# DRAM copies of the inverse transform's rows laid out by output quarter, each quarter loaded by two or four transfers

## The chip, the cores and the metric

The kernel runs on one NeuronCore of a Trainium2 chip. The metric is the device time of one execution in microseconds (us). Its engines are TensorE (PE; weight loads are listed apart as PEld), VectorE (DVE), ScalarE (ACT), GpSimd (POOL) and SyncE (SP), which here only issues DMAs. POOL also issues some. The transfers of both are carried by the same 16 DMA engines.

## The reference

Two independent computations, whose outputs lie side by side in one (1, 2048, 1280) bf16 tensor.

Part A is a local attention: 32 heads of width 20, each position attending to 8 positions at distances 0, 2, ..., 14.

```python
qkv = (x @ wqkv).reshape(B, S, 3, H, Dh)
logits = einsum("bhsd,bhswd->bhsw", q, kg) * scale    # kg, vg: rows gathered at pos - 2*w
attn = softmax(where(mask, logits, -1e9))
a = einsum("bhsw,bhswd->bhsd", attn, vg).reshape(B, S, D) @ wo
```

Part B is a long convolution, done by Fourier transforms, with a kernel that is generated from the parameters, and a skip term:

```python
K = einsum("dn,dnl,dn->dl", Cc, exp(logdA[:, :, None] * l), dB).real
y = irfft(rfft(u, padded to 2L) * rfft(K, padded to 2L))[:L]
b = y + u * Dskip
```

## The kernel before, in words

Part B's 640 channels are five chunks of 128 (`NCH = 5`, index c). The outer loop of `body` runs over c. In each turn DVE, PE and ACT generate one chunk's convolution kernel (four `unit`s), while the chunk before goes through its transform (`transform`), the product with the input's spectrum (`products`, L357) and the first half of the inverse transform (`inverse_a`, L373). The second half is done for all channels at the end, by the class `Inverse` (L653).

Between the two halves the data go through DRAM, since the second half needs the rows in another order:

- `inverse_a` has a tile Z of 128 partitions x 4096 bf16 for chunk c; after its fourth piece SP issues one DMA (L386) that writes it to `Zd[c]`, 8 KB in a row for each partition. A row is (real or imaginary, l0, ut), and l0 has 64 values, of which a *quarter* is 16.
- `times_d` (L391), ten times, multiplies half a chunk of the input by the skip factor on DVE and SP writes it to `UDd[c]` (L397), 2 KB in a row for each partition.
- `Inverse.load(qr, c0, c1)` (L666) fills the tile of quarter qr: 96 partitions (32 real, 32 imaginary, 32 skip rows) x 4 groups g x 5 chunks x 16 l0 x 32. For every chunk it issues three DMAs of 128 KB, each to 32 partitions, in rows of 1 KB: fifteen for a quarter. For quarters 0 and 3 they alternate between SP and POOL (8 and 7), for quarters 1 and 2 all go to SP.
- `Inverse.part` (L676) takes 2 or 3 values of l0: PE multiplies the quarter's rows by the table HB into `ps_ib`, ACT copies that to a row buffer `ysb` (four of them), and after every eighth l0 SP writes the buffer out in four DMAs (L690). There are 24 parts, six for a quarter.

A planner orders the instructions of each engine by modelled costs, except where the program pins them: `keep_in_program_order`, `issue_after`, and, from `att.in_order()` (L833) on, every matmul and ACT copy. Each engine then works its list in order; what it needs from others it waits for on semaphores. The transfers that SP issues take eight semaphores in turn.

The end of the program, from about 353 us, is a hand-written order: six `GROUPS` (L845) of eight steps `av_step` (L608), the attention-weighted sum over V. In each step DVE makes a product and PE adds it up in `ps_o`. Between the steps lie parts of the inverse, pieces of the output projection (`out_piece`, L631), and the loads of quarters 2 and 3, which `LOADS` (L846) puts at step numbers 8 * group + w: one chunk at each of the steps 4, 6, ..., 22. Parts 12 to 17 use quarter 2, parts 18 to 23 quarter 3, and the first of these stand in group 2 (step 21) and group 3 (step 31).

The tiles of the quarters take over space: quarter 0 a pool that opens when the transform's pool closes, quarter 1 the space of kT (free after the last `products` of the attention), quarter 2 that of `prod`, quarter 3 that of xT (free after the last `proj_v`).

Of the kernel before, what the change touches and what calls it, by code (L numbers as in the profile page):

```python
# [13 lines left out]
bf16 = mybir.dt.bfloat16  # L14
f32 = mybir.dt.float32

NCH = 5
# [355 lines left out]
def inverse_a(tc, pools, C, P1, P2, Zd, pool):  # L373

    nc = tc.nc
    MM = nc.tensor.matmul
    Z = pool.tile([128, 128, 32], bf16, name="Z", tag="sp", bufs=3)

    def piece(b):
        ps = pools["psum"].tile([128, 8, 128], f32, name="ps_ia", tag="bank2")  # L380
        for j in range(8):
            for w, P in enumerate((P1, P2)):
                MM(ps[:, j], lhsT=P[:, 8 * b + j].rearrange("p k g -> p (k g)"), rhs=C["EA"][:, w, :], start=(j % 4 == 0 and w == 0), stop=(w == 1), skip_group_check=True)
        nc.scalar.copy(out=Z[:, :, 8 * b:8 * b + 8], in_=ps[:].rearrange("p j x -> p x j"))
        if b == 3:
            nc.sync.dma_start(out=Zd, in_=Z[:].rearrange("p x j -> p (x j)"))  # L386

    return [lambda b=b: piece(b) for b in range(4)]


def times_d(tc, pools, C, UDd, c, i):  # L391

    nc = tc.nc
    U = C["U"][:].rearrange("p l (ut c) -> p c l ut", c=NCH)[:, c]
    UD = pools["tabb"].tile([128, 32, 32], bf16, name="UD", tag="UD")
    tc.keep_in_program_order(nc.vector.tensor_tensor(out=UD[:], in0=U[:, 32 * i:32 * i + 32], in1=bc(C["Dsb"][:, c], 1, 32), op=A.mult))
    nc.sync.dma_start(out=UDd[c, :, 1024 * i:1024 * i + 1024], in_=UD[:].rearrange("p l j -> p (l j)"))  # L397


def fwd_u(tc, pools, C, Sd, c):  # L400
# [252 lines left out]
class Inverse:  # L653
# [12 lines left out]
    def load(self, qr, c0=0, c1=NCH):  # L666
        nc = self.nc
        pool, tag = ((self.a2, "Z"), (self.att.ta, "LPC"), (self.att.a1, "prod"), (self.att.ta, "U"))[qr]
        if c0 == 0:
            self.t[qr] = pool.tile([96, 4, NCH, 16, 32], bf16, name="Z", tag=tag)  # L670
        for c in range(c0, c1):
            for ri in range(3):
                src = self.UDd[c, :, 512 * qr:512 * qr + 512] if ri == 2 else self.Zd[c, :, 2048 * ri + 512 * qr:2048 * ri + 512 * qr + 512]
                (nc.sync, nc.gpsimd)[(c + ri) % 2 if qr in (0, 3) else 0].dma_start(out=self.t[qr][32 * ri:32 * ri + 32, :, c].rearrange("p g l n -> p g (l n)"), in_=src.rearrange("(g p) n -> p g n" if ri == 2 else "(p g) n -> p g n", g=4))

    def part(self, l0, n):  # L676
        nc = self.nc
# [18 lines left out]
def body(tc, ctx, pools, prm, B_u, B_Dskip, Sd, Zd, UDd, A_x, A_wqkv, A_wo, out_a, out_b):  # L696
    nc = tc.nc
# [4 lines left out]
    fp = fft.enter_context(tc.tile_pool(name="fft", bufs=1, side="right"))  # L702
# [51 lines left out]
    LAST = NCH - 1  # L754
    for c in range(NCH):
        Kb[c] = (fp, pools["tabb"])[c % 2].tile([128, 32, 64], bf16, name="Ksb", tag="Ksb")
        F, G, Xs = small_half(tc, pools, B["cT"][:, c], R[c], *trig[c, 0][:2], 0)
        if c > 0:
            transform(c - 1)
        trig[c, 1] = trig_half(tc, pools, B, c, 1)  # L760
        unit(c, 0, 0, F, G, Xs[0])
        if c > 0:
            P1, P2, last = products(tc, pools, Sk[c - 1], Sd[c - 1], fp, True)
            ia = inverse_a(tc, pools, C, P1, P2, Zd[c - 1], fp)
            ia[0]()
        unit(c, 0, 1, F, G, Xs[1])
        if c > 0:
            for f in ia[1:]:
                f()
        if c < LAST:  # L770
            last_u = fwd_u(tc, pools, C, Sd, c if c == 0 else c + 1)
            if c == 0:
                first_u = last_u
        if c == LAST:
            att.open_k()
            for ct in range(5):
                att.proj_k(0, ct)
            att.k_halo()
        with ExitStack() as order:
            if c > 0:  # L780
                order.enter_context(tc.issue_after(last.ins))
            F, G, Xs = small_half(tc, pools, B["cT"][:, c], R[c], *trig[c, 1][:2], 1)
        if c < LAST:
            with tc.issue_after(trig[c, 1][2].ins):
                B["coefficients"](c + 1, psg)
                R[c + 1] = exps_chunk(tc, pools, B, c + 1)
            trig[c + 1, 0] = trig_half(tc, pools, B, c + 1, 0)
        else:
            att.open_q0()
        with ExitStack() as order:  # L790
            if c == 0:
                order.enter_context(tc.issue_after(first_u.ins))
            unit(c, 1, 0, F, G, Xs[0])
        if c == 0:
            fwd_u(tc, pools, C, Sd, 1)
        unit(c, 1, 1, F, G, Xs[1], q_first if c == LAST else lambda: None)
        if c == LAST - 1:
            att.load_x()
# [9 lines left out]
        if w == 3:  # L808
            transform(LAST)
    P1, P2, _ = products(tc, pools, Sk[LAST], Sd[LAST], fp, False)  # L810
    ia = inverse_a(tc, pools, C, P1, P2, Zd[LAST], fp)
    att.softmax_a(0)
    for ct in range(5):
        att.proj_q(1, ct)
# [4 lines left out]
    fft.close()  # L819
    a2 = ctx.enter_context(tc.tile_pool(name="a2", bufs=1, side="right", reuse_waits="tile"))  # L820
    inv = Inverse(att, a2, Zd, UDd, out_b)
    inv.load(0)
    att.open_v()
    for w in range(W):
        if w >= 2:
# [17 lines left out]

    att.open_out(a2)
    GROUPS = ((0, 256, 0, 2, None), (0, 128, 2, 3, 0), (128, 128, 2, 3, 1), (256, 128, 0, 4, None), (256, 256, 4, 1, 2), (384, 128, 0, 4, 3))  # L845
    LOADS = {4 + 2 * n: (2 + n // NCH, n % NCH) for n in range(2 * NCH)}  # L846
    for group, (i0, ni, j0, nj, done) in enumerate(GROUPS):
        for w in range(W):
            if group == 0:
                fill(parts, (0, 2, 0, 2, 0, 1, 0, 1)[w])  # L850
                if w == 3:
                    att.exp(1)
                if w in (0, 3):
                    att.proj_v(16 + 2 * (w == 3))
                if w == 5:
                    att.v_halo(8, 12)
            att.av_step(i0, ni, j0, nj, w)
            if 8 * group + w in LOADS:
                qr, c = LOADS[8 * group + w]
                inv.load(qr, c, c + 1)  # L860
            if 8 * group + w in (6, 8, 11, 14):
                n = (6, 8, 11, 14).index(8 * group + w)
                att.sums(2 * n, 2 * n + 2)
            if group == 0:
                if w == 2:
                    att.softmax_a(1)
                elif w == 7:
                    att.open_wo()
            elif group == 1:
                if w in (3, 5, 7):  # L870
                    fill(parts, 2)
            elif group == 2:
                if w == 1:
                    fill(rest, 3)
                elif w == 3:
                    att.reciprocal()
                    att.softmax_b(1)
                    fill(rest, 5)
                elif w in (5, 7):
                    fill(parts, 2)  # L880
            elif group < 5:
                if w % 2 == 1:
                    fill((rest, parts)[w // 2 % 2], 2)
            elif w % 2 == 1:
                fill(rest, 2)
        if done is not None:
            rest += att.out_proj(done, done == 3)
# [4 lines left out]
@with_exitstack  # L892
def kernel(
    ctx: ExitStack,
    tc: tile.TileContext,
    A_x: bass.AP,
    A_wqkv: bass.AP,
    A_wo: bass.AP,
    B_u: bass.AP,
    B_A_re: bass.AP,  # L900
    B_A_im: bass.AP,
    B_B_re: bass.AP,
    B_B_im: bass.AP,
    B_C_re: bass.AP,
    B_C_im: bass.AP,
    B_log_dt: bass.AP,
    B_Dskip: bass.AP,
    out: bass.AP,
):
    nc = tc.nc  # L910
    prm = dict(B_A_re=B_A_re, B_A_im=B_A_im, B_B_re=B_B_re, B_B_im=B_B_im, B_C_re=B_C_re, B_C_im=B_C_im, B_log_dt=B_log_dt)
    out_a = out[0][:, 0:640]
    out_b = out[0][:, 640:1280]
    pools = {}
    pools["const"] = ctx.enter_context(tc.tile_pool(name="const", bufs=1))
    idc = nc.inline_tensor(np.eye(128, dtype=np.float32).astype(ml_dtypes.bfloat16), name="ident_c")
    ident = pools["const"].tile([128, 128], bf16, name="ident")
    nc.sync.dma_start(out=ident[:], in_=idc.ap())
    pools["ident"] = ident
    dpool = ctx.enter_context(tc.tile_pool(name="dram", bufs=1, space=bass.MemoryType.DRAM))  # L920
    Sd = dpool.tile([NCH, 128, 4096], bf16, name="Sdram")
    Zd = dpool.tile([NCH, 128, 4096], bf16, name="Zdram")
    UDd = dpool.tile([NCH, 128, 2048], bf16, name="UDdram")
    body(tc, ctx, pools, prm, B_u, B_Dskip, Sd, Zd, UDd, A_x, A_wqkv, A_wo, out_a, out_b)


# [28 lines left out]
```

## Time and profile before

| | |
|---|---|
| median of three runs | 427.67 us (426.81 to 433.45) |
| the profiled execution | 426.76 us, of which the span of the profile is 425.0 us |
| busy in the span | PE 351.9, PEld 261.5, DVE 379.0, ACT 312.0, POOL 39.1 us |
| DMA | 51.76 MB in 45280 packets, mean 122 GB/s |
| loads of the quarters | SP 30 + 16, POOL 10 + 4, of 128 KB each |
| writes behind them | 5 of 1024 KB (`Zdram<-Z`), 10 of 256 KB (`UDdram<-UD`) |

Instants are us from the span's start. A line of the timeline gives start, duration, engine, source line, operation and tiles, how many instructions were merged (x4), and in brackets how long the engine had been idle before, with what ended that. SPq is SP's list of DMA instructions: the duration there is that of issuing, not of the transfer. All matmuls from L833 on carry the line of one helper, L429, and are told apart by their tiles.

### The profile page before, as it was taken

Reading aid. Unit: us, or ns where it says so; the run is one execution under the profiler, and the core shown is the slowest. Engines: PE = TensorE matmul, PEld = TensorE weight load, DVE = VectorE, ACT = ScalarE, POOL = GpSimd, SP = SyncE. Lnnn points to the kernel's source line nnn. Section 1 sums busy time; section 2 is a strip of 40 time slices with the busy share of each in tenths; the row PEclk is TensorE's granted clock in tenths of the full one; section 3 lists DMA queues with packets and bytes.
Section 4 is the critical chain, followed back from the end, with each engine's and each line's share of the span. In section 5 each row is a group of like instructions: output and inputs, shape, how many; then the busy total and the mean of one; then the engine's idle time right before and its main releaser. Section 6 shows DMA issues by size and latency. Waiting matters only on the chain. (4 is left out here: it accounts for less than half of the span.)

```text
span 425.0 us, 18968 instructions
## 1 busy us (share of the span) xinstructions
PE 351.9 (83%) x8693; PEld 261.5 (62%) x8693; DVE 379.0 (89%) x353; ACT 312.0 (73%) x574; POOL 39.1 (9%) x83
## 2 busy tenths in 40 slices
PE   1294769979996989969897799999799989879795
PEld 0183668867974778758785677545545666445353
DVE  7899997998997999999996989855987999999671
ACT  3984989789999999979998684433757545656552
POOL 7430000000000000000010000100000300502120
PEclk9998668999999898978997899999999999999899
DMA  5579103073233402334079942600040553887542
GB/s 148 166 174 201 25 3 126 29 244 83 102 128 127 100 29 103 143 110 102 29 274 239 217 102 93 231 2 3 2 100 2 175 114 108 239 218 203 158 127 93
DMA packets 45280, 51.76 MB, mean 122 GB/s; under 512 B 31392, under 2 KB 39136, under 8 KB 42512
## 3 DMA queue, kind: packets, MB, share of 16 engines
q1 hardware_dynamic: 41664, 41.47, 35.8%
q0 software_dynamic: 3392, 8.95, 7.2%
q8 instruction: 68, 1.11, 1.1%
q10 hardware_dynamic: 144, 0.12, 0.1%
q14 instruction: 12, 0.10, 0.1%
HBM read 28.08 MB, written 18.35 MB: 109 GB/s over the span
## 5 line engine op out<-in xcount | busy, mean ns | idle before, releaser
L312 DVE TENSOR_TENSOR Y<-PG 128x3072 bf16<-128x3072 bf16 x60 | 103.1, 1752 | 5.6 <-PE ps_k L330 5.5
L258 PE MATMUL ps_ph<-LPC 128*64 128x256 bf16 x400 | 43.7, 317 | 16.0 <-DMA LPC<-lo 8.7
L325 PE MATMUL ps_k<-Y,X 128*32 128x64 bf16 x1920 | 46.9, 239 | 8.6 <-issue 4.7
L330 PE MATMUL ps_k<-Y,X 64*32 64x64 bf16 x1920 | 44.6, 233 | 3.8 <-issue 3.8
L353 ACT CAST Sg<-ps_f 128x1024 bf16<-128x1024 f32 x40 | 37.7, 1038 | 7.7 <-PE ps_f L352 7.7
L325 PEld LDWEIGHTS <-X 128*32 128x32 bf16 x1920 | 32.2, 117 | 17.9 <-issue 9.7
L232 ACT ACTIVATE R<-LPC 128x192 bf16<-128x192 f32 x155 | 41.9, 387 | 0.0
L345 ACT CAST A<-ps_f 128x1024 bf16<-128x1024 f32 x40 | 38.0, 1045 | 2.6 <-PE ps_f L344 2.6
L330 PEld LDWEIGHTS <-X 64*32 64x32 bf16 x1920 | 30.0, 113 | 13.2 <-issue 5.3
L352 PE MATMUL ps_f<-A,T 128*64 128x128 bf16 x640 | 28.8, 265 | 10.8 <-ACT A L345 9.8
L282 DVE TENSOR_TENSOR X<-R,TX 128x1536 bf16<-128x1536 bf16 x40 | 37.2, 951 | 0.0
L258 PEld LDWEIGHTS <-LPC 128*64 128x64 bf16 x400 | 21.7, 122 | 21.7 <-issue 16.9
L266 ACT ACTIVATE TX<-ps_ph 128x768 bf16<-128x768 int16 x40 | 29.8, 837 | 6.9 <-DVE X L282 5.2
L352 PEld LDWEIGHTS <-T 128*64 128x64 bf16 x640 | 27.1, 141 | 12.4 <-issue 12.1
L618 DVE TENSOR_TENSOR prod<-v,atp 128x2048 bf16<-128x2048 bf16 (+2 forms) x32 | 30.8, 1020 | 3.5 <-PE ps_o L429 3.5
L266 ACT ACTIVATE TA<-ps_ph 128x768 bf16<-128x768 int16 x40 | 30.1, 818 | 1.4 <-PE ps_ph L262 1.4
L262 PE MATMUL ps_ph<-LPC 128*64 128x128 bf16 x400 | 29.0, 240 | 0.0
L429 PE MATMUL ps_op<-wo,o 128*128 128x320 bf16 x160 | 24.9, 307 | 1.6 <-ACT ob L430 0.9
L262 PEld LDWEIGHTS <-LPC 128*64 128x64 bf16 x400 | 24.5, 126 | 0.8
L367 DVE TENSOR_TENSOR P<-P,Sg 128x4096 bf16<-128x4096 bf16 x10 | 22.9, 2285 | 2.0 <-DMA P<-Sdram 1.6
L531 DVE TENSOR_TENSOR prod<-qT,kT 128x1024 bf16<-128x1024 bf16 (+1 forms) x16 | 23.0, 1483 | 0.5 <-ACT qT L499 0.5
L282 DVE TENSOR_TENSOR PG<-R,TA 128x3072 bf16<-128x3072 bf16 x10 | 17.5, 1752 | 6.5 <-ACT TA L266 6.5
(132 smaller groups left out, 663.9 us busy)
## 6 DMA issues: line engine op xcount, KB each, us to landing
Sdram<-Sg SPq DMA_DIRECT2D x5, 1024.0 KB
P<-Sdram SPq DMA_DIRECT2D x5, 1024.0 KB
P<-Sdram SPq DMA_DIRECT2D x10, 512.0 KB
Zdram<-Z SPq DMA_DIRECT2D x5, 1024.0 KB
Z<-Zdram SPq DMA_DIRECT2D x30, 128.0 KB
U<-in_B_u_dram SPq DMA_DIRECT2D x4, 640.0 KB
UDdram<-UD SPq DMA_DIRECT2D x10, 256.0 KB
out_dram<-ysb SPq DMA_DIRECT2D x32, 80.0 KB
```

The source lines that it names most:

```text
L232: nc.scalar.activation(out=RX[:, :, e - 16, :], in_=src, func=ACT.Exp, scale=m)
L258: MM(o[64 * hh:64 * hh + 64, :, 0:8], lhsT=L[:, 64 * hh:64 * hh + 64], rhs=rhs, start=first, stop=last, skip_group_check=True, tile_positi ...
L262: MM(o[64 * hh:64 * hh + 64, :, 8:12], lhsT=L[:, 128:192], rhs=rhs[:, :, 16 * hh:16 * hh + 16], start=False, stop=last, skip_group_check=T ...
L266: last = nc.scalar.activation(out=dst, in_=words.rearrange("p b (q e f) -> p b q (e f)", e=8, f=4), func=ACT.Sin, scale=PI_LO / 32768.0)
L282: TT = lambda o, a, b, op: V.tensor_tensor(out=o, in0=a, in1=b, op=op)
L312: nc.vector.tensor_tensor(out=Y[:].rearrange("p q (b a) f -> p q b a f", a=8), in0=fa, in1=gb, op=A.mult)
L325: MM(ps[32 * g:32 * g + 32, t], lhsT=X[:, q, k, :, f], rhs=Ys[k][:, q, :, f], start=(t == 0 and k == 0), stop=False, tile_position=(0, 32 ...
L330: MM(ps[32 * g:32 * g + 32, t], lhsT=X[hb, q, k, :, f], rhs=Ys[k][hb, q, :, f], start=False, stop=(k == 2), tile_position=(64 * (g // 2), ...
L345: nc.scalar.copy(out=A1[:, :, 32 * b:32 * b + 32].rearrange("p k (j g) -> p k j g", g=4), in_=ps[:].rearrange("p j k g -> p k j g"))
L352: last = MM(ps[sl, kk], lhsT=C["T2"][:, 8 * b + kk, sl], rhs=A1[:, 8 * b + kk, :], start=(kk % 4 == 0), stop=True, skip_group_check=True, ...
L353: nc.scalar.copy(out=Sg[:, :, 8 * b:8 * b + 8, :], in_=ps[:].rearrange("p k (j g) -> p j k g", g=4))
L618: ins = nc.vector.tensor_tensor(out=p2.rearrange("p (d i) -> p d i", i=ni), in0=self.v2[:, 4 * j0:4 * j0 + 4 * nj, off:off + ni], in1=at[: ...
```

## The change

The two DRAM tensors get the quarter as a dimension outside the chunk, so that for one row and one quarter all chunks lie side by side. Every write and load of them follows:

- `Zd` is written by two DMAs for each chunk instead of one (real, imaginary), and both it and `UDd` in rows of 1 KB instead of 8 KB and 2 KB.
- `load` issues two DMAs for any range of chunks, both on SP: the skip rows (32 partitions), then the real and imaginary rows together (64 partitions). A row of the transfer is as long as the range: 5 KB for five chunks.
- Quarter 0 is loaded as chunks 0 to 3 and then chunk 4, quarter 1 in one range. Quarters 2 and 3 are loaded as chunks 0 to 2 and 3 to 4, at the steps 4 and 9, and 14 and 19.

```diff
@@ inverse_a
         if b == 3:
-            nc.sync.dma_start(out=Zd, in_=Z[:].rearrange("p x j -> p (x j)"))
+            for ri in range(2):
+                nc.sync.dma_start(out=Zd[ri].rearrange("p g q n -> (p g) q n"), in_=Z[:, 64 * ri:64 * ri + 64].rearrange("p (q l) j -> p q (l j)", q=4))
@@ times_d
-    nc.sync.dma_start(out=UDd[c, :, 1024 * i:1024 * i + 1024], in_=UD[:].rearrange("p l j -> p (l j)"))
+    nc.sync.dma_start(out=UDd[:, :, 2 * i:2 * i + 2, c].rearrange("g p q n -> (g p) q n"), in_=UD[:].rearrange("p (q l) j -> p q (l j)", q=2))
@@ Inverse.load
-        for c in range(c0, c1):
-            for ri in range(3):
-                src = self.UDd[c, :, 512 * qr:512 * qr + 512] if ri == 2 else self.Zd[c, :, 2048 * ri + 512 * qr:2048 * ri + 512 * qr + 512]
-                (nc.sync, nc.gpsimd)[(c + ri) % 2 if qr in (0, 3) else 0].dma_start(out=self.t[qr][32 * ri:32 * ri + 32, :, c].rearrange("p g l n -> p g (l n)"), in_=src.rearrange("(g p) n -> p g n" if ri == 2 else "(p g) n -> p g n", g=4))
+        for r0, nr, src in ((64, 32, self.UDd[:, :, qr, c0:c1].rearrange("g p c n -> p g (c n)")), (0, 64, self.Zd[:, :, :, qr, c0:c1].rearrange("r p g c n -> (r p) g (c n)"))):
+            nc.sync.dma_start(out=self.t[qr][r0:r0 + nr, :, c0:c1].rearrange("p g c l n -> p g (c l n)"), in_=src)
@@ body
-            ia = inverse_a(tc, pools, C, P1, P2, Zd[c - 1], fp)
+            ia = inverse_a(tc, pools, C, P1, P2, Zd[:, :, :, :, c - 1], fp)
...
-    inv.load(0)
+    inv.load(0, 0, LAST)
+    inv.load(0, LAST)
...
-    LOADS = {4 + 2 * n: (2 + n // NCH, n % NCH) for n in range(2 * NCH)}
+    LOADS = {4: (2, 0, 3), 9: (2, 3, NCH), 14: (3, 0, 3), 19: (3, 3, NCH)}
...
             if 8 * group + w in LOADS:
-                qr, c = LOADS[8 * group + w]
-                inv.load(qr, c, c + 1)
+                inv.load(*LOADS[8 * group + w])
@@ the kernel's head
-    Zd = dpool.tile([NCH, 128, 4096], bf16, name="Zdram")
-    UDd = dpool.tile([NCH, 128, 2048], bf16, name="UDdram")
+    Zd = dpool.tile([2, 32, 4, 4, NCH, 512], bf16, name="Zdram")
+    UDd = dpool.tile([4, 32, 4, NCH, 512], bf16, name="UDdram")
```

## The prediction, made before the changed kernel was run

> **What bounds the kernel now.** I read the page's busy rows, then the chain that ended last, then the waits of DVE and PE after 320 us, then the timelines of PE, DVE and SP around the one wait that a load ends.
>
> ```profile
> span 425.0 us, 18968 instructions
> PE 351.9 (83%) x8693; PEld 261.5 (62%) x8693; DVE 379.0 (89%) x353; ACT 312.0 (73%) x574; POOL 39.1 (9%) x83
> 415.53 5.96 PE ps_op L429 x40
> ```
>
> DVE is nearest to a bound. The chain of waits reaches back only to 415.49 us, the last output projection; what is ahead of that must be read from the waits. Of 353 to 412 us, the stage with the loads, DVE is idle for 3.48 us, in two places that PE ends; PE's longest idle there ends on a DMA:
>
> ```profile
> DVE prod L618 <- PE ps_o L429: 3.5, 2, 1.9
> PE ps_ib L429 <- DMA out_dram<-ysb: 3.0, 1, 3.0
> 394.55 0.65 PE L429 MATMUL ps_o<-atp,ident 32*32 32x512 bf16 x32
> 398.16 0.96 PE L429 MATMUL ps_ib<-Z,HB 96*32 96x160 bf16 x24 [2.96 <-DMA out_dram<-ysb]
> 399.64 2.50 PE L429 MATMUL ps_op<-wo,o 128*128 128x320 bf16 x10
> 399.60 1.29 DVE L618 TENSOR_TENSOR prod<-v,atp 128x1024 bf16<-128x1024 bf16 x2 [1.86 <-PE ps_o L429]
> 402.51 2.36 DVE L618 TENSOR_TENSOR prod<-v,atp 128x2048 bf16<-128x2048 bf16 x2 [1.62 <-PE ps_o L429]
> ```
>
> The matmuls at 398.16 are parts 18 and 19, the first to read quarter 3, in PE's pinned order. The output write named as releaser is nothing that they read; by the trace's landing events the last load of quarter 3 landed at 397.33, within the wait, so I put the wait down to it. Why it landed so late is on SP:
>
> ```profile
> 372.31 4.02 SPq L690 DMA_DIRECT2D out_dram<-ysb x4
> 376.43 2.06 SPq L674 DMA_DIRECT2D Z<-Zdram  x2
> ...
> 387.14 2.76 SPq L690 DMA_DIRECT2D out_dram<-ysb x4
> 389.94 2.38 SPq L674 DMA_DIRECT2D Z<-Zdram  x2
> 392.37 0.59 SPq L674 DMA_DIRECT2D Z<-UDdram  x1
> 393.00 1.19 SPq L674 DMA_DIRECT2D Z<-Zdram  x2
> 394.23 0.59 SPq L674 DMA_DIRECT2D Z<-UDdram  x1
> ```
>
> From 353.48 to 394.82 SP issues 38 loads of 128 KB and 16 output writes with hardly a pause, about 0.55 to 0.6 us each and up to 1.6. The last load belongs to step 22, which DVE reaches near 383 (steps 20 to 23 begin at 381.48, 0.89 us each), and goes out at 394.23: SP is some 11 us behind. Part of that is the rotation of eight semaphores: the writes at 372.95, 374.70 and 376.02 start within 0.02 us of the landing of the transfer eight places before them.
>
> **Part by part.** *Fewer loads on SP.* In that stage SP's 38 loads become 2 + 4 + 4 = 10, and POOL's 7 go. SP's saving is 28 x 0.59 = 16.5 us, more than its lag. Quarter 3's first piece stands at step 14, behind the output writes of part 8 (`ysb` ready at 375.4, four writes at 0.5 us): issue near 377.5. Its last piece stands at step 19, behind the writes of part 11 (ready at 380.1): issue near 382, two at 0.6 to 1.6 us. The data are 1.18 MB and then 96 rows x 4 x 2 KB = 0.79 MB; at the 231 GB/s of the stretch 367 to 385 that is 5.1 us, to about 384, and 3.4 us. With the 2 to 4 us that a load there takes when little is ahead of it (the last ones: 3.1 from issue to landing), the last piece lands at 388 to 391, and PE wants it at 395.2. The wait of 2.96 us goes; at least 4 us are the margin, used up at 157 GB/s instead of 231 (8.5 us become 12.5).
>
> *What is then late next.* PE gains 2.96 us. It gains more by its clock: the granted clock is 0.67 in the stretch 399 to 403 and 1.00 in 403 to 412; ten `ps_op` matmuls take 2.50 us there against 1.52 at 393.10, and 24 of `ps_ib` 0.96 against 0.60 at 386.68: 1.34 us, together 4.3. The Trainium skill, "TensorE: Matmul & The Clock Gate", its rules for kernel authors, says to avoid idle gaps of PE above about 3 us, since the clock then falls to half; the trace agrees with one such gap, 2.96 us, and the low clock behind it. By the rule the low clock goes with the gap (4.3 us on PE), by the bare idle time 2.96. DVE can regain only its idle 3.48 us; it ran without a gap before, from 353 to 397. The stage's end is thus earlier by 2.96 to 3.48 us; I take 3.2, since PE and DVE are level there (two steps with an output piece are 2.18 us on PE, 2.31 on DVE). From 412 on nothing in the chain reads the changed data: PE, ACT and the last writes move as one block.
>
> *The first quarter.* Its last chunk goes through `Zd` just before: the write was issued at 333.44 and landed at 338.79, the last load landed at 347.01, and PE reads the quarter at 359.4 after working without a wait on it until 359.05 (the 0.33 us named for it there I take as nothing). Cover: 12 us. The change takes away rows of 8 KB (median 315 ns a packet in the trace, 128/16 x 315 = 2.5 us a chunk) and writes 1 KB rows (46 ns, 1024/16 x 46 = 2.9 us), adds one issue of 0.33 us, and puts the seven loads that POOL issued in SP's list. The planner may also see the strided pieces as overlapping and hold the load of chunks 0 to 3 until the write lands; then 1.97 MB start at 339.5 and, at the 169 GB/s of the stretch 329 to 340, land by 351. Cost nothing; 8 us of cover stay.
>
> *A rule on ports against the merged rows.* Packets of 1 KB took 46 ns at the median and 62 in the mean, so a quarter's 1920 packets need 5.5 to 7.4 us of 16 engines; those of 5 KB (POOL's, elsewhere) took 196 to 240 ns, 384/16 x 196 to 240 = 4.7 to 5.8 us. The Trainium skill, "SBUF — State Buffer", section "Door 1: The DMA port swizzle", states that partitions 0 to 63 reach no more ports than 0 to 31, 218 GB/s at most, so an estimate from that page is 6.0 us for the 1.31 MB of `Zd` alone and 9.0 with the skip rows in series. No row separates the two here. By either, quarter 3 is there before 395.2, and the sum stays.
>
> *Quarters 1 and 2.* Quarter 1 goes out at 353.48 as before (it waits for kT), in 2 issues instead of 15 that lasted until 363.99; it landed at 367.06 and is used at 372.45: 5 us of cover, growing. Quarter 2's last load landed at 386.36, used at 386.68: only 0.3 us of cover. It now has its last loads at step 9, behind the writes of part 5 (`ysb` ready at 368.3): issued near 370.5, so some 8 us more. The tile for quarter 3 needs xT, free at 363.4, long before step 14.
>
> *Writes earlier on.* Five more issues (0.33 us) on SP, which there waits for tens of us, and `UD` rows of 1 KB instead of 2 KB (256/16 x 46 = 0.74 against 128/16 x 85 = 0.68 us). Queued behind them on SP are the write and reloads of `Sd`; in the whole trace one DVE wait of 1.60 us hangs on those, at 315.11, 51 us after the `Zd` write before it. Nothing. POOL without its 14 loads has nothing else waiting: its output writes wait for ACT.
>
> **The sum.** 426.76 - 3.2 = 423.6 us against the profiled execution (span 425.0, to 421.8). The median of three runs lies 0.9 above that execution, and 427.67 - 3.2 = 424.5; I say 424.0.
>
> **Rivals.** *A, nothing is gained:* something else holds PE or DVE at the same place, such as ACT, which empties `ps_ib` and `ps_o`. For: ACT ended three waits of PE on `ps_ib` (1.4 us). Against: ACT is busy 2.20 of 4 us in 395 to 399. Gain 0 to 1: 426 to 428. Chance 0.13.
>
> *B, slower, by the first quarter:* DRAM writes of 1 KB rows with 4 KB gaps between take so long that quarter 0 lands after 359. Every us beyond is one of PE in its pinned order. It decides from 12 us beyond today's 347; slower than before needs 15, so a write of some 20 us instead of 5.35, and 2% needs 24. No packet row suggests a factor of four. 436 us and more; chance 0.03.
>
> *C, another plan:* the order of instructions ahead of 353 us is planned from modelled times, and the writes of `Zd` return a buffer of the ring of three that A1, Sg, P1, P2 and Z share. If the model sees a chunk's write end later, transforms or products move behind other work, five times. A slip exposes one reload of `Sd`, 4.5 to 7.0 us from issue to landing in the trace. It outweighs the gain of 3.2 from one exposed reload on, and is over 2% from three: 424 + 3 x 4.5 = 437.5. With one or two: 428.5 to 433. For: little pins PE and ACT there. Against: the writes landed 3.9 to 5.4 us after their issue and PE was idle for the tile Z's sake for 0.9 us in all, so little hangs on it. Chance 0.14, of which 0.10 over 2%.
>
> *D, another plan that is shorter:* of DVE's 46 us without work (425.0 - 379.0) 26.7 lie between 60 and 353 us (40 - 36.45 and 253 - 229.85 in the stretches' table); to gain 2% a new order must find 5.4 of them beyond the 3.2. Chance 0.09, time 412 to 419.
>
> **How the numbers follow.** Forecast 0.61, A 0.13, B 0.03, C 0.14, D 0.09. Two per cent of 427.67 is 8.6 us, about what a measurement of this kernel can tell from no change (its three runs spread over 6.6). Faster by over 2%: D, 0.09. Within: forecast, A and the smaller C, 0.78. Slower by over 2%: B and the rest of C, 0.13. The forecast alone spans 422.4 (426.76 less PE's 4.3) to 424.7 (427.67 less 2.96); the range takes in A and the smaller C, and 2 us below for a median that falls with D's lesser forms: 420.5 to 431.
>
> **What would show it.** Right: ten SP loads after 353 us; quarter 3's last issue near 382 to 384 instead of 394; no PE wait near 395; DVE without a gap from 353 to its last step near 408; granted clock 1.00 in the stretch after. Wrong: a PE wait ended by ACT in that place (A), by quarter 0's loads near 359 (B), or DVE reaching 353 us at another instant (C, D): the stage ahead of 353 should keep its length to 1 us.

## The result, and the profile after

The changed kernel takes 434.85 us (median of four runs, 432.84 to 435.88) against 428.76 for the kernel before beside it (four runs, 426.81 to 433.45): a ratio of 1.0125 with a 95% interval of 1.0083 to 1.0167. It is slower by 1.25%, some 5.4 us, where 424.0 was forecast and 431 was the end of the range. The profiled execution took 435.83 us. That of before, 426.76, was among the quick ones: in the comparisons further down the kernel before had medians of 429.4 to 430.6, with single runs from 424.7 to 435.6. So of the 9.1 us between the two profiles a part is scatter. Some executions are slow ones, whatever the kernel: the medians of the experiments count them, the ratios leave them out, and the profiles of e2, e6 and e9 are of such executions, so that no span and no stage of theirs is compared.

The page's first lines:

```profile
span 434.1 us, 18914 instructions
PE 354.4 (82%) x8693; PEld 259.9 (60%) x8693; DVE 379.1 (87%) x353; ACT 311.7 (72%) x574; POOL 31.5 (7%) x69
```

PE, DVE and ACT have the same instructions as before, in the same order; DVE is as busy (379.1 against 379.0). Only the lists of SP and POOL differ. DVE comes to the first step of the end stage at 356.79 instead of 353.32, and from there to the end of the span it is 77.3 us instead of 71.7: 5.6 more, about what the ratio says. (The instant at which the stage begins scatters from 352.9 to 361.4 over the profiles of this study, though PE, DVE and ACT work the same lists ahead of it.)

**DVE.** Its waits in the stage, from 353 to 415 us (what waits, for whom; total, times, longest):

```profile
DVE prod L619 <- PE ps_o L430: 2.8, 2, 1.6
DVE tree L578 <- PE ps_s L430: 2.4, 1, 2.4
DVE atp L619 <- PE ps_o L430: 2.0, 1, 2.0
DVE prod L619 <- ACT v L431: 1.4, 1, 1.4
```

The first line answers to the 3.5 us of before and is 0.7 us less. The other three are new: 1.40 + 2.01 + 2.36 = 5.8 us. Where they lie, and what PE did ahead of them, on the timelines of DVE and then of PE:

```profile
372.00 3.56 DVE L619 TENSOR_TENSOR prod<-v,atp 128x1536 bf16<-128x1536 bf16 x4 [1.40 <-ACT v L431]
382.79 1.83 DVE L619 TENSOR_TENSOR atp<-v,atp 128x1536 bf16<-128x1536 bf16 x2 [2.01 <-PE ps_o L430]
386.98 1.76 DVE L578 RECIPROCAL tree<-ps_s 128x256 f32<-128x256 f32 x1 [2.36 <-PE ps_s L430]
```

```profile
364.09 0.38 PE L430 MATMUL ps_o<-prod,ident 32*32 32x512 bf16 x3
366.18 0.43 PE L430 MATMUL ps_o<-prod,ident 32*32 32x512 bf16 x13 [1.71 <-issue]
367.14 3.77 PE L430 MATMUL ps_v<-xT,wv 128*32 128x512 bf16 x40
...
378.66 0.25 PE L430 MATMUL ps_ib<-Z,HB 96*32 96x160 bf16 x3
380.95 0.38 PE L430 MATMUL ps_ib<-Z,HB 96*32 96x160 bf16 x9 [2.04 <-issue]
384.87 2.08 PE L430 MATMUL ps_s<-lsb,tree 128*128 128x256 f32 x4
...
406.95 0.60 PE L430 MATMUL ps_ib<-Z,HB 96*32 96x160 bf16 x24
```

The same groups in the kernel before, whole and without a stop ahead of them:

```profile
360.14 0.42 PE L429 MATMUL ps_o<-prod,ident 32*32 32x512 bf16 x16
361.14 2.35 PE L429 MATMUL ps_v<-xT,wv 128*32 128x512 bf16 x40
...
372.45 0.39 PE L429 MATMUL ps_ib<-Z,HB 96*32 96x160 bf16 x12
...
376.03 1.13 PE L429 MATMUL ps_s<-lsb,tree 128*128 128x256 f32 x4
```

In the changed kernel PE stops twice in the middle of a group of equal matmuls, 3 + 13 and 3 + 9, for 1.71 and 2.04 us, and the releaser is "issue": the profile shows nothing that it waits for. The `ps_v` matmuls behind the first stop run at half clock (3.77 us instead of 2.35 for the same 40), so ACT gets v late, and DVE waits 1.40. The second stop makes `ps_o` late by 2.01, and four `ps_s` matmuls at half clock take 2.08 instead of 1.13. The wait of before at 395 is gone: parts 18 and 19 start at 406.95 with no bracket.

The stretches (window; length, then busy time and instructions of PE, PEld, DVE, ACT, POOL; granted clock, DMA share, GB/s), of the kernel after and then of the kernel before:

```profile
376.00:386.00 10.00, 6.60 (x151) 3.89 (x151) 6.60 (x8) 2.46 (x5) 0.00 (x0) 0.88 1.06 222
386.00:395.00 9.00, 8.15 (x122) 3.75 (x121) 7.99 (x7) 3.57 (x7) 0.57 (x1) 0.56 0.96 205
```

```profile
376.00:386.00 10.00, 8.50 (x160) 5.32 (x144) 9.97 (x9) 5.77 (x12) 1.53 (x3) 1.00 0.77 206
386.00:395.00 9.00, 8.43 (x278) 4.35 (x276) 9.00 (x10) 6.16 (x13) 1.23 (x3) 1.00 0.78 212
```

After, the 16 DMA engines are busy all the time in these two stretches, though they move hardly more; before, they had a quarter of the time free there.

**What "issue" is.** PE's instructions come by DMA too. The page's list of queues has them (packets, MB, share):

```profile
q8 instruction: 68, 1.11, 1.1%
```

PE has 8693 + 8693 = 17386 matmuls and weight loads, and 17386 / 256 = 67.9: one packet of 16 KB for every 256 records. Its "issue" idle times of 0.9 us and more lie nearly all at one place of such a block of 256, and end 1.2 to 1.6 us after a packet of q8 has ended. Numbering the packets and taking a block's border as every 256th record, one sees that packet k goes with the crossing of border k, and that PE does not pass border k + 1 before it has come. Border crossings and packets, read from the trace (us; "after" is the packet's start less the crossing, and "PE stood" runs from the start of the last record of a block to that of the next, so it is some 0.3 us more than the idle time on the timeline):

```
                 crossed  packet starts  after   ends   next border  PE stood
before   57       354.63     354.46      -0.2   355.80    359.96       0
         59       364.94     367.53       2.6   368.61    371.93       0
         60       371.93     376.20       4.3   377.45    379.30       0
         64       394.80     398.96       4.2   400.04    403.04       0
after    55       346.44     350.56       4.1   351.84    352.26       1.04
         57       358.99     363.23       4.2   364.56    364.10       2.08
         59       372.06     378.13       6.1   379.48    378.66       2.28
         60       380.95     385.47       4.5   386.79    388.90       0
```

With little else on the DMA engines a packet starts within about 1 us of the crossing and takes about 1 us. Behind the merged loads it starts 4 to 6 us late, and PE, which needs 4 to 9 us for a block in this stage, runs dry where the block is short. Before, two packets are as late (60 and 64), but ahead of blocks of 7.4 and 8.2 us; the first of them falls into a stretch, 368 to 376 us, in which the DMA engines were full there too (share 1.07). As an estimate, 4 to 6 us are the time of ten to fifteen of the load's 5 KB packets on one engine at the 396 ns measured below. Crossing 55 lies in the loads of quarter 0, 57 in that of quarter 1, 59 in that of quarter 2, beside POOL's load of `wo`.

**SP's list and the ports.** SP, in the same stretch (start, issuing time):

```profile
356.95 0.31 SPq L673 DMA_DIRECT2D Z<-UDdram  x1
357.31 0.51 SPq L673 DMA_DIRECT2D Z<-Zdram  x1
367.46 2.61 SPq L689 DMA_DIRECT2D out_dram<-ysb  x4
370.18 0.41 SPq L673 DMA_DIRECT2D Z<-UDdram  x1
370.63 0.52 SPq L673 DMA_DIRECT2D Z<-Zdram  x1
```

SP is idle for most of the time now, as forecast, but quarter 1, two instructions, lands only at 368.58, 11.3 us after the second was issued. Its packets of 5 KB took 386 ns (skip rows) and 396 ns (real and imaginary rows) at the median, against 196 ns at the median (240 in the mean) for such packets elsewhere in the trace of before; 16 engines at 396 ns a packet make 207 GB/s. The Trainium skill, "SBUF — State Buffer", section "Door 1: The DMA port swizzle", puts rows in partitions 0 to 63 on the ports of 0 to 31, 218 GB/s at most; the trace agrees with these 207.

### The profile page after: what moved, and what is told of

Its sections match the earlier page's. It is cut to its first block, busy times and chain, and to the rows that moved or that the text cites. A ratio compares the mean times of both kernels' runs of the same rounds, so it can differ in the third digit from the quotient of the medians.

```text
span 434.1 us, 18914 instructions
## 1 busy us (share of the span) xinstructions
PE 354.4 (82%) x8693; PEld 259.9 (60%) x8693; DVE 379.1 (87%) x353; ACT 311.7 (72%) x574; POOL 31.5 (7%) x69
## 5 line engine op out<-in xcount | busy, mean ns | idle before, releaser
L258 PE MATMUL ps_ph<-LPC 128*64 128x256 bf16 x400 | 41.9, 306 | 17.2 <-DMA LPC<-lo 8.7
L352 PE MATMUL ps_f<-A,T 128*64 128x128 bf16 x640 | 26.4, 251 | 12.2 <-ACT A L345 10.5
L258 PEld LDWEIGHTS <-LPC 128*64 128x64 bf16 x400 | 20.9, 118 | 23.4 <-issue 9.9
L352 PEld LDWEIGHTS <-T 128*64 128x64 bf16 x640 | 24.8, 132 | 13.8 <-issue 13.6
L430 PE MATMUL ps_op<-wo,o 128*128 128x320 bf16 x160 | 25.9, 315 | 2.6 <-ACT ysb L431 1.7
L262 PEld LDWEIGHTS <-LPC 128*64 128x64 bf16 x400 | 23.6, 121 | 0.7
L331 ACT CAST Ksb<-ps_k 128x512 bf16<-128x512 f32 x20 | 11.6, 590 | 17.2 <-PE ps_k L330 17.2
```

The lines of the kernel that those rows point to most:

```text
L258: MM(o[64 * hh:64 * hh + 64, :, 0:8], lhsT=L[:, 64 * hh:64 * hh + 64], rhs=rhs, start=first, stop=last, skip_group_check=True, tile_positi ...
L262: MM(o[64 * hh:64 * hh + 64, :, 8:12], lhsT=L[:, 128:192], rhs=rhs[:, :, 16 * hh:16 * hh + 16], start=False, stop=last, skip_group_check=T ...
L352: last = MM(ps[sl, kk], lhsT=C["T2"][:, 8 * b + kk, sl], rhs=A1[:, 8 * b + kk, :], start=(kk % 4 == 0), stop=True, skip_group_check=True, ...
```

## The experiments

With the result three causes were open: the new layout in DRAM (writes in rows of 1 KB), the merging of loads (issued faster than carried, in long bursts), and the half of the ports that the merged rows reach. Beside them stood the doubt whether the wait that went was worth 3.2 us at all. Ratios are to the kernel before in the same comparison, with 95% intervals.

### The layout alone (e1)

The changed layout and writes, with the fifteen loads of before for each quarter, from the new tensors:

```diff
-        for r0, nr, src in ((64, 32, ...), (0, 64, ...)):
-            nc.sync.dma_start(...)
+        for c in range(c0, c1):
+            for ri in range(3):
+                src = self.UDd[:, :, qr, c] if ri == 2 else self.Zd[ri, :, :, qr, c]
+                (nc.sync, nc.gpsimd)[(c + ri) % 2 if qr in (0, 3) else 0].dma_start(...)
```

What was expected of e1:

> The changed kernel's DRAM layout and writes (Zd by two DMAs a chunk, rows of 1 KB), but the loads of before: 15 DMAs of 128 KB a quarter, 32 partitions each, at the same steps and queues. Theory F (PE's instruction fetches wait behind the long loads at the end, and PE stands at a block border until they land): the loss comes from the loads, so 427 to 429 us here, ratio to before 0.998 to 1.003, no stall of PE named issue of over 1.5 us between 353 and 400 us, the wait of about 3 us at quarter 3 back. Rival W (the writes in short rows cost the 3 us that the changed kernel had lost by 275 us): 430 to 432, ratio 1.006 or more, DVE's first step of the attention sum (353.3 in before) at 356 or later.

Measured: 428.63 us, 0.9964 [0.9923, 1.0005]; from the first step to the end 70.9 us. The layout costs nothing that can be measured, so the cost of the change is in its loads. And a second thing: with the load list of before, parts 18 and 19 hardly wait,

```profile
397.05 0.60 PE L430 MATMUL ps_ib<-Z,HB 96*32 96x160 bf16 x24 [0.27 <-issue]
```

0.27 us instead of the 2.96 of the first profile.

### Loads by chunk, and the ports (e2, e3, e8, e12)

e2 merges the rows but not the chunks: two DMAs for a chunk, rows of 1 KB, at the steps of before.

```diff
-    LOADS = {4: (2, 0, 3), 9: (2, 3, NCH), 14: (3, 0, 3), 19: (3, 3, NCH)}
+    LOADS = {4 + 2 * n: (2 + n // NCH, n % NCH) for n in range(2 * NCH)}
...
-    inv.load(0, 0, LAST)
-    inv.load(0, LAST)
+    for c in range(NCH):
+        inv.load(0, c, c + 1)
...
-    inv.load(1)
+    for c in range(NCH):
+        inv.load(1, c, c + 1)
```

What was expected of e2:

> The changed kernel, but each quarter loaded chunk by chunk (two DMAs a chunk, 32 and 64 partitions, rows of 1 KB, ten a quarter, all on SP), quarters 2 and 3 at the steps of before. Theory F: the transfers come at the pace of SP's issues (about 197 KB in 1.1 us) instead of 1.3 MB at once, so a fetch finds gaps; the fetch waits of over 4 us in 353 to 400 us fall to under 3 and the two stalls of 2 us go: 425 to 429 us. Rival P (what counts is that 64 partitions in one transfer reach half of the SBUF's ports): the 64-row transfers are as many bytes as before, packets of 1 KB take 70 ns or more, stalls stay: 431 to 435. Rival W: not under 430.

Measured: 429.14 us, 0.9992 [0.9951, 1.0034]: the loss is gone. Packets still start up to 3.6 us late, where under 3 was expected, and one stop of PE of over 1 us is left, behind crossing 62:

```profile
PE ps_op L430 <- issue: 1.7, 1, 1.7
```

e3 keeps the change whole and moves the rows: skip rows at partitions 0 to 31, real and imaginary at 32 to 95, which by the section of the Trainium skill named above ("SBUF — State Buffer", "Door 1: The DMA port swizzle") reach twice as many ports as 0 to 63; the table HB is put together in the same order.

```diff
-    HB = np.concatenate([2 * np.cos(psi) / 4096, -2 * np.sin(psi) / 4096, np.broadcast_to(np.eye(32)[:, None, :], (32, 64, 32))], 0)
+    HB = np.concatenate([np.broadcast_to(np.eye(32)[:, None, :], (32, 64, 32)), 2 * np.cos(psi) / 4096, -2 * np.sin(psi) / 4096], 0)
...
-        for r0, nr, src in ((64, 32, self.UDd[...]), (0, 64, self.Zd[...])):
+        for r0, nr, src in ((0, 32, self.UDd[...]), (32, 64, self.Zd[...])):
```

What was expected of e3:

> The changed kernel, but the skip rows stand at partitions 0 to 31 and the real and imaginary rows at 32 to 95 (the table's rows in the same order), so that the one long load covers partitions of both halves. Same DMAs, sizes, steps. Rival P, or F with P as the reason why the bursts last so long: packets of 5 KB in quarter 1's load take about 200 to 240 ns instead of 380 to 398, the load lands 2 to 3 us earlier, the fetch behind it waits 2 us or less instead of 4.2, its stall shrinks or goes; 427 to 431 us. Theory F without P (a burst blocks a fetch for as long as its bytes are queued, ports or not): packets as before, 433 to 435. Rival W alone: 433 to 435 too, with the stalls in the end unchanged.

Measured: 431.19 us, 0.9975 [0.9939, 1.001], against 1.0125 for the same kernel with the other row order. The load of quarter 1, as GB/s in 40 slices of the window 357 to 369 us, of the kernel after and of e3:

```profile
GB/s 0 0 51 273 17 85 273 393 273 222 171 239 222 205 222 205 256 239 239 205 191 239 205 222 119 239 256 188 205 188 222 188 171 154 72 0 17 41 186 37
```

```profile
GB/s 0 0 0 119 137 68 208 119 375 341 222 188 205 222 222 256 188 256 393 341 427 375 410 393 427 393 154 123 34 160 134 29 19 32 193 138 169 164 226 102
```

From the eleventh slice on both run at some 220, e3 with its skip rows (387 ns a packet, as after); then e3 goes to 340 to 430, and its bytes have moved by 365, while the kernel after stays near 220 until 366.6 and ends by 367.5. Packets of the real and imaginary rows take 201 ns at the median instead of 396. No packet of instructions starts more than 3.7 us late in this stage, and PE stands at a border for 0.3 us at most.

What was expected of e12:

> e3 once more (the changed kernel with its 64 rows at partitions 32 to 95), to set it closer beside before, e7 and e11: ratio 0.992 to 0.999 and no stall over 1 us at a block border after 350 us. If e3's profile without stalls was chance: a stall of over 1 us there, ratio over 1.002.

The same kernel on another chip: 428.19 us, 0.9973 [0.9937, 1.0009]. No stop at a border is over 0.6 us. From the first step to the end it is 70.5 us in the one profile and 69.9 in the other.

e8 is e2 with the rows of e3:

What was expected of e8:

> e2 (loads by chunk, two DMAs each, rows of 1 KB, on SP) with the row order of e3: the candidate for a version better than both. Fetch waits under 3 us in the last stage, no stall there over 1 us, quarter 3's last load down by 395 us (3 us ahead of PE's need) and no wait for it: stretch from the first attention step to the end 69.5 to 70.5 us, ratio 0.993 to 0.998. If SP's issues (20 loads by chunk for quarters 2 and 3 and 16 writes) still are late: a wait of 1 us or more near quarter 3 and ratio 0.998 to 1.002.

Measured: 431.29 us, 1.0007 [0.9974, 1.004], not the 0.993 to 0.998 expected of the candidate. Where no long burst is, the row order moves nothing that can be measured. PE stood 0.85 us behind crossing 62.

### The forecast gain alone (e4)

The kernel before, with the loads of quarter 2 shared between SP and POOL, which takes the lag from SP and touches no layout and no row length:

```diff
-                (nc.sync, nc.gpsimd)[(c + ri) % 2 if qr in (0, 3) else 0].dma_start(...)
+                (nc.sync, nc.gpsimd)[(c + ri) % 2 if qr in (0, 2, 3) else 0].dma_start(...)
```

What was expected of e4:

> The kernel before, with one word changed: quarter 2's loads alternate between SP and POOL as those of quarters 0 and 3 do, so that SP issues 7 fewer of the 38. The first step of the prediction alone (SP is late for quarter 3, PE waits 2.96 us and then runs at half clock for 3.4): SP is 4 us earlier with quarter 3, its last load lands by 394, the wait goes, and the time is 423 to 425.5, ratio 0.990 to 0.995. If PE's time there is bound by something else as well: 426 to 428.

Measured: 431.08 us, 1.0027 [0.999, 1.0064]. The wait of 2.96 us is not in its profile, the stage to the end takes 70.3 us instead of 71.7, and yet the time does not fall. At crossing 58 the packet starts 3.7 us late and PE stands 1.34 us, so e4 does not show the relief of SP by itself: the loads that POOL now issues in the same time brought a stop, as it seems.

### The change again (e5)

What was expected of e5:

> The changed kernel itself, for a closer ratio and a second profile beside e6 to e8. Theory F: ratio 1.006 to 1.013, and again one or more stalls of PE at an instruction block's border (record 193 or 194 modulo 256) of 1 to 2.3 us between 344 and 400 us after its start of the stage, each behind a fetch that waited 4 us or more, and half clock after it. If the stalls of the first profile were chance: ratio under 1.004 and none over 1 us.

Measured: 433.98 us, 1.0101 [1.0061, 1.0142]. The same three crossings fail: 55, 57 and 59, with packets 4.2, 4.7 and 5.1 us late, and PE stands 1.05, 2.63 and 1.43 us. From the first step to the end it is 75.9 us. The stops belong to the kernel and not to one execution.

### One burst, in two row orders (e6, e7)

This is the pair that isolates the cause. Both are e1 with quarter 1 alone merged into two DMAs of 5 KB rows; e7 differs from e6 only in the order of the rows (in all four quarters, and in the table).

```diff
+        if qr == 1:
+            for r0, nr, src in ((64, 32, ...), (0, 64, ...)):    # e7: (0, 32, ...), (32, 64, ...)
+                nc.sync.dma_start(...)
+            return
         for c in range(c0, c1):
```

What was expected of e6:

> e1 (layout and writes of the change, loads of before) with one load changed: quarter 1 in two DMAs of 0.66 and 1.31 MB, as in the changed kernel. Theory F: the fetch that PE asks for within the 10 us of this burst waits 4 us or more, PE stands 1 to 2.3 us at the border that follows, and the stretch from the first step of the attention sum to the end grows by 1 to 3 us over e1 (70.9 us); ratio 1.000 to 1.004. If one burst alone does no harm (only the later ones, beside the output writes and the wo load, do): no fetch wait over 3 us there, stretch 70.5 to 71.5, ratio as e1 (0.996).

What was expected of e7:

> e6 with the rows of the tiles in another order (skip rows at partitions 0 to 31, real and imaginary at 32 to 95), all else equal. Rival P: the burst lands some 1.5 to 2.5 us sooner than in e6 (packets of the 64-row load near 200 ns instead of 390), and the fetch within it waits 1 to 2 us less, so at most 1 us of stall. Theory F without P: fetch wait and stall as in e6.

Measured: e6 434.39 us, 1.0069 [1.0016, 1.0122]; e7 428.48 us, 0.9928 [0.9887, 0.997]. The intervals do not touch. PE's timeline in e6, and the same matmuls in e7:

```profile
371.09 0.40 PE L430 MATMUL ps_o<-prod,ident 32*32 32x512 bf16 x4
372.80 0.43 PE L430 MATMUL ps_o<-prod,ident 32*32 32x512 bf16 x12 [1.32 <-issue]
...
380.92 0.39 PE L430 MATMUL ps_ib<-Z,HB 96*32 96x160 bf16 x12 [1.46 <-issue]
```

```profile
370.32 0.44 PE L430 MATMUL ps_o<-prod,ident 32*32 32x512 bf16 x16
...
377.84 0.39 PE L430 MATMUL ps_ib<-Z,HB 96*32 96x160 bf16 x12
```

The group of 16 is cut into 4 + 12 by the stop, and the next border stops PE again. In both kernels PE crosses border 58 at 6.49 us after the first of the two loads was issued (366.14 - 359.65, and 365.37 - 358.88). In e6 the load runs until 371.81, and the packet starts 4.05 us late; in e7 it ends at 368.51, and the packet starts 1.29 us late. e7 has 3.4 us of half clock in the stage; the two profiles of the changed kernel have 13.6 and 10.2.

e7 is the only kernel here whose interval lies below 1; it overlaps those of e1, e3 and e12, so that it is better than they are is not shown.

### Two merged quarters (e11)

e7 with quarter 2 merged as well, at step 4, and quarter 3 by chunks from step 6 on:

```diff
-        if qr == 1:
+        if qr in (1, 2):
...
-    LOADS = {4 + 2 * n: (2 + n // NCH, n % NCH) for n in range(2 * NCH)}
+    LOADS = {4: (2, 0, NCH), **{6 + 2 * n: (3, n, n + 1) for n in range(NCH)}}
```

What was expected of e11:

> A candidate: e7 with quarter 2 in one range too (at step 4, two DMAs, the 64 rows at partitions 32 to 95), quarter 3 by chunks at the steps 6 to 14 on SP and POOL, quarter 0 as before. SP has 13 loads fewer than e7, so quarter 3 lands by 392 and its wait goes for good: stretch from the first attention step to the end 69 to 70 us, ratio 0.990 to 0.995. If the second burst, beside the wo load and the output writes, holds up a fetch: a stall of 1 us or more near 375 to 382 and 0.996 to 1.002.

Measured: 431.01 us, 1.0057 [1.0012, 1.0102], worse than e7: the intervals do not touch. Quarter 2 lies beside the load of `wo` and output writes; the packets at crossings 59 and 60 start 5.1 and 5.2 us late, and PE stands 0.38 and 1.55 us. So the better row order is not enough where a whole quarter in one range shares the engines with other transfers. In e3 and e12, where quarter 2 comes in two ranges, packet 59 was 3.7 us late and PE did not stand.

### A burst without use (e9, e10)

e1 with one copy of the size and row length of the real and imaginary rows, from xT into a part of `Sd` that is read no more, behind the loads of quarter 0: from partitions 0 to 63 (e9) and 32 to 95 (e10).

```diff
+    with tc.issue_after(inv.last.ins):
+        nc.sync.dma_start(out=Sd[...], in_=att.xT[0:64]...)    # e10: att.xT[32:96]
```

What was expected of e9:

> e1 plus one transfer that nobody waits for: right behind quarter 0's loads SP copies 1.31 MB of xT (partitions 0 to 63, rows of 5 KB) to a part of the DRAM scratch tensor that is no longer read. It follows quarter 0's loads in the queue, so it runs at about 346 to 353 us, where SP, and no other engine, has a wait of 12 us. Theory F: the fetch that PE asks for within it (near 348) waits 3 to 5 us instead of 0.4, and PE stands up to 2 us at the next border (near 354); quarter 1's loads begin on a DMA queue that is free again. Ratio 0.997 to 1.003 (e1 0.996). If PE stood in the changed kernel for data and not for its instructions: fetch wait under 1.5 us, no stall, ratio as e1.

What was expected of e10:

> e9 with the copy taken from partitions 32 to 95 instead, the same bytes and rows. With P: packets near 200 ns instead of 390, the transfer over 3 us sooner (by 350), the fetch wait 1 to 3 us shorter than in e9, no stall over 1 us there. Without P: as e9.

Measured: e9 429.06 us, 0.9985 [0.9941, 1.0028]; e10 429.68 us, 0.9967 [0.9919, 1.0015]. Packets took 387 ns in e9 and 196 in e10, so the ports count in this direction too. But no stop came: the copy of e9 ran from 352.5 to 359.0, PE crossed only border 56 in it, at 356.8, when little more than 2 us of it were left, and the packet started 1.7 us late. The 3 to 5 us expected there did not come; the experiment missed its place and says nothing for or against the cause.

## Why the prediction was wrong, step by step

**The step that failed: the price of the merged rows.** The prediction weighed the packets of 5 KB, with 4.7 to 5.8 us by the rows and 9.0 by its estimate from the Trainium skill ("SBUF — State Buffer", "Door 1: The DMA port swizzle"), and closed: "By either, quarter 3 is there before 395.2, and the sum stays." The longer time was the nearer one (quarter 1's packets lasted 10.2 us from the first to the last), and the load was still early enough for its reader. But it asked only whether the data come in time. A burst that keeps the engines full also holds up what else they carry, here PE's own instructions. No rival held that. e6 against e7 shows it, with nothing but the row order between them: 1.0069 against 0.9928. How the load holds a packet of instructions up stays open: that it queues behind the load's packets is inferred from the starts of both, and the trace does not show the queue of a DMA engine.

**The term that was mis-sized: 3.2 us for the wait on quarter 3.** Its working named the right wait, and the change removes it. But its size was that of one execution, and the wait is not worth its length. In the profiles that issue quarters 2 and 3 as before does, by chunk at the same steps, the same matmuls waited 2.96 us (before), 0.27 (e1 and e7) and 0.53 (e10), and 0.27 and 4.66 in e6 and e9. From the first step to the end it is 69.5 to 70.9 us in e1, e3, e7, e10 and e12, which have little or nothing of the wait and no stop at a border over 0.6 us, against 71.7: 0.8 to 2.2 us less, where 3.2 was put. On the time of the kernel even less is clear: e4, which takes the lag alone, gained nothing (1.0027), and the whole change without the ports' cost gained a quarter of a per cent, some 1.1 us, with an interval that holds 1 (e3, e12). Only one execution of the kernel before was profiled, so how often it has the long wait is not known.

**The sum then.** Some 1 us won, not clear of nothing (e3, e12), and some 6 lost: the ratio of the change is 1.0125, that of e3, the same with the other row order, 0.9975. Of this loss the stops behind crossings 57 and 59 are 2.08 and 2.28 us in the profile; what the stop behind crossing 55, ahead of the stage's first step, and the additional half clock take was not separated. From the first step to the end the profile has 5.6 us more than before's, and the ratio says 5.4.

**Fewer loads on SP:** right. Ten loads in the stage. In e3, which has no stops, the last went out at 386.31 and landed at 392.5; its stage began 3.7 us later than before's, and less that the two are 382.6 and 388.8, both within the forecast (382 to 384, 388 to 391). In the kernel after they are 392.17 and 399.4, or 388.7 and 395.9 less the 3.5 us by which its stage began later: the stops held the steps up. Cover was enough in both: no wait.

**The clock:** the low clock at 398 went with its gap, as forecast, and came back elsewhere: half clock for 3.4 us from 366.6 and for 10.2 us from 383.7. The rule cited (the Trainium skill, "TensorE: Matmul & The Clock Gate", section "Why this matters for your kernels": no idle gaps of PE above some 3 us) was taken for the whole condition. The traces differ: it came behind gaps of 1.71 and 2.04 us too, and of the kernels without a stop of over 0.3 us at a border in this stage e3 and e7 have 3.4 us of it and e1 6.8. What sets it off is not settled here.

**The first quarter, "cost nothing":** right for its reader (landed at 351.8, no wait), so rival B falls. But its loads stopped PE for 1.04 us at crossing 55. "Quarters 1 and 2": the cover held.

**Writes earlier on:** right, by e1.

**Rivals C and D, another plan:** fall. The instruction lists of PE, DVE and ACT are the same, in order, in every kernel of this study. **Rival A, nothing gained:** its gain of 0 to 1 us is about what the relief of SP was worth on the time (e4, e3 and e12), though no wait for ACT explains it; the change as a whole came out slower than that.

**What would show it:** three of the signs of being right held, though the time did not: ten loads, no wait of PE near the old one, and a granted clock of 1.00 in the stretch that had been slow (395 to 412 us). The last issue was late, and the sign that led to the cause was DVE, named as running without a gap: its three new waits lead straight to PE's stops. One sign of being wrong misled: DVE reached its first step 3.5 us later than before, which was to stand for another plan (C, D), but the plan is the same and that instant scatters by more than this from profile to profile.

## What to carry to other kernels

Before merging small DMAs into large ones, ask what else the DMA engines carry at that time, PE's own instructions among it: PE idle for "issue" in the middle of a group of equal instructions was the sign here. A merged load did no harm where its packets ran at 201 ns and little else was on the engines (e7), and it did harm at 396 ns (e6) or beside other loads (e11); fifteen small transfers paced by their issue can be the kinder ones. And a wait seen in one profile is priced by more than one execution before it goes into a sum.

## What the runs showed of the hardware

PE gets its instructions 256 at a time, in packets of 16 KB that come by DMA, about one block ahead, as the table above shows. Where the packet starts within 1.2 us of the crossing, it takes some 3.5 us from there until the next block can run (about 1 us to the packet's start, 1 to 1.4 for the packet, 1.4 until PE goes on). Where PE works off a block in less, it stands at nearly every border: ahead of the end stage there are blocks of 2.4 us, and the stops over 0.3 us between crossings 6 and 54 add up to 15.2 us in the profile of before and to 19.4 and 16.2 in the two of the kernel after, with 20.9 in that of e4. The later start of the end stage goes with a larger sum, though loosely (352.9 us with 16.5 in e1, 356.7 with 20.9 in e4). Nothing in this study was tried against those stops.

The row order is a matter of one line: 32 skip rows first, 64 others from partition 32 on, halves the packet time of the larger transfer (201 against 396 ns), which agrees with the section "Door 1: The DMA port swizzle" of the Trainium skill's page "SBUF — State Buffer", by which the half of the ports is chosen by whether a row lies below or from 64 on.
